# Gated attention and mixer on one core: the queues of the first loads, transposes for the first outputs, and the share of mixer work at the end

## The chip, the cores and the metric

The kernel runs on one core of a Trainium2 chip. The metric is device time in microseconds (us) from start to end of one execution. TensorE (PE) multiplies matrices and writes to the accumulation memory (PSUM); VectorE (DVE) and ScalarE (ACT) work element by element; GpSimd (POOL) and SyncE (SP) here mostly issue transfers. Transfers (DMAs) are issued on the queues of SP, ACT and POOL and all run on the same 16 DMA engines. Each engine works through its own instructions in order, and waits on semaphores for those of others.

## What is computed

Eight batches, each with 3136 rows; u and v have 256 columns, z has 64. All inputs and the output are float32.

```
attn = max(z z^T / S, 0)^2          # 3136 x 3136, symmetric
x    = u * (attn v)                 # gate
h    = V^T (U^T x)                  # low-rank mix over the rows, rank 32
u2   = x + h
out  = u2 + max(u2 w1, 0) w2        # w1: 256 x 1024, w2: 1024 x 256
```

The first two lines are called attention here, the others the mixer. `moe_U`, `moe_V`, `moe_w_ch1` and `moe_w_ch2` are U, V, w1 and w2.

## The kernel before

Rows are cut into 24 blocks of 128 and a tail of 64 (index 24). A score block (i, j) is a 128 x 128 product of z columns (line 881), two running at once in the two halves of TensorE's rows. ScalarE or VectorE applies the relu on the way from PSUM to SBUF (lines 896, 898; 1024 columns at a time as a rule), and VectorE squares it in place (902). Output block c sums 25 products of a score block with a v block (909) in one of two PSUM accumulators (`NACC = 2`), then VectorE multiplies by u (935, "the gate"). The tail's output is summed transposed (917) and turned (927).

The scores are symmetric, so from batch 1 on only blocks with j >= i are computed, and the others are made by a transposing DMA from SBUF to SBUF on SP's queue (905), up to 8 blocks each. In batch 0, where the transposes would come late, the columns 0 to 7 are computed for all rows without transposes (`DIRECT = 8`), and the triangle with transposes begins at column 8. The tail's scores (tile TJ) are always transposed: 12 blocks that each of the outputs 0 to 23 needs once.

The mixer of a batch: t1 = U^T x over the whole batch (944), a copy, then for each of seven groups k of rows (six of 512, a tail): h (963), add (974), cast (755 or 753), a transposing DMA (991), w1 in four parts of 256 columns (1001), relu (1012 on ScalarE, 1014 on VectorE), w2 in two halves of 16 products (1027), add (1039) and a store from POOL's queue (1044). Two output buffers `ob` take turns.

Nothing of this order is written out by hand. `make_plan` lists tasks with engines they may run on, durations, dependencies, buffers to take and priorities, and `Plan.run` plays them through once, at build time; the order in which the tasks start there is the order of the instructions on each engine. A task with two engines goes to the first unless that is behind by more than its `slack`. `behind` means "not before that one has started". `select` chooses TensorE's next task: score blocks up to `LOOK` outputs ahead in bursts, else the next products of an output, else mixer work. Mixer work is taken when its progress lies more than one batch and `HOLD` = 0.12 of a batch behind that of attention.

Start of batch 0: z is loaded by SP and ACT, v by SP and POOL in turn, each v load of two blocks (256 KB) into one of six staging buffers `stg`, from where VectorE or ScalarE casts it to bf16. The first u loads (for outputs 0 to 5 and the tail) and all weight loads go out on POOL's queue: two weight loads after the gate of each of the first six outputs in order, w1 first, then w2, U and V. They are cast from the staging buffers too. The first t1 waits for all weights.

Of the kernel before, what the change touches and what calls it, by code (L numbers as in the profile page):

```python
# [15 lines left out]
P = 128  # L16
NB, S, D, DQK, R, H = 8, 3136, 256, 64, 32, 1024
NT = 24
# [8 lines left out]
DIRECT = 8  # L27
HOLD = 0.12

# [246 lines left out]
def make_plan():  # L276
# [9 lines left out]
    duos, avs = [], []  # L286
    out_done = {}
    after = lambda b, pos: out_done.get((b, pos))
    wts = []
# [6 lines left out]
    for b in range(NB):  # L296
# [45 lines left out]
        for n, k in enumerate([12] + list(range(12))):  # L342
            st = Ref("stg")
            w = 2 if k < 12 else 1
            ld = add(
                f"vld{b}.{k}", {"ACT": 0.5} if b else {("SP", "POOL")[k % 2]: 0.55},
# [36 lines left out]
        tail = [(place[0], True, None, 0), (place[0], True, None, 16)]  # L383
        direct = 0
        if b == 0:

            for s in range(0, DIRECT, 4):
                at = place[s]
                for j in range(s, NT, 2):
                    units.append((at, False, [(j, s, 4), (j + 1, s, 4)]))  # L390
                if s == 0:
                        units += tail
                for c in range(s, s + 4):
                    units += [(place[s + 4], False, x) for x in split(c, s + 4, NT - s - 4)]
            direct = DIRECT
        else:
            units = tail
        for c in range(direct, NT):
            units += [(place[c], True, x) for x in split(c, c, NT - c)]
        small = []  # L400
        for at, turn, parts, *j0 in units:
            al = []
            if parts is None:
# [9 lines left out]
            else:  # L413
# [11 lines left out]
                nt = (t0 + len(tiles) - r0) if turn else 0  # L425
# [21 lines left out]
            if nt:  # L447
                src = [TJ] if parts is None else [refs[r0 - t0 + i] for i in range(nt)]
                x = add(
                    f"tr{b}.{c}.{t0}", {"SP": t_tr(nt)},  # L450
                    lambda K, t, src=src, tb=tb, nt=nt, o=t0 * 64: K.tr_quad(t, src[0], o, tb, nt),
                    deps=[s], prio=0.5, pipe=T_BLK * nt, use=src + tb.refs,
                )
            for n, (r, i) in enumerate(tiles):
                sq[r, i] = s
                if parts is not None:
                    row[r, i] = blk.refs[n]
                    if nt and i >= r0:
# [14 lines left out]
        xs, evs = [], []  # L473
        for pos, c in enumerate(order):
            if c == NT or c % 2 == 0:
                u = Ref("u24" if c == NT else "us")
                uld = add(
                    f"uld{b}.{c}", {"ACT": 0.5} if b or pos > 6 else {"POOL": 0.55}, lambda K, t, b=b, c=c, u=u: K.load_u(t, b, c, u),
                    deps=[after(b, pos - 6) if pos > 6 else after(b - 1, 18 + pos)], prio=3.5, behind=[] if b else vl[-1:],
# [11 lines left out]
            acc = Ref("acc")  # L491
            last, at = None, 0
            for i, seg in enumerate(groups):
# [6 lines left out]
                emit = lambda K, t, seg=seg, acc=acc, v=v, f=first, l=end: K.av(t, seg, acc, v, f, l)  # L500
                if c == NT:
# [4 lines left out]
                    alloc=[acc] if first else [], use=list(refs.values()) + [v] + ([] if first else [acc]),  # L506
                )
                last.b, last.pos, last.n = b, b * 25 + pos, len(seg) * (0.27 if c == NT else 1.0)
# [17 lines left out]
            elif c > 0:  # L526
                x = xs[-1]
            takes = c == NT or c % 4 == 0
            ev = add(
                f"x{b}.{c}", {"DVE": t_dvp(P if c == NT else D)},  # L530
                lambda K, t, c=c, acc=acc, u=u, x=x: K.gate(t, c, acc, u, x),
                deps=[last, uld] + ([] if takes else [evs[-1]]), prio=0.2,
                alloc=[x] if takes else [], use=[acc, u] + ([] if takes else [x]),
            )
            out_done[b, pos] = ev
            evs.append(ev)

            for n in range(2 * pos, min(2 * pos + 2, 12)) if b == 0 else ():
                st = Ref("stg")
                ld = add(  # L540
                    f"wld{n}", {"POOL": 0.6}, lambda K, t, n=n, st=st: K.load_w(t, n, st),
# [559 lines left out]
```

## Time and profile before

| | us |
|---|---|
| median of 5 executions | 1062.05 |
| lowest and highest | 1057.31, 1063.96 |
| the profiled execution | 1063.64 |
| its span, first to last instruction | 1060.7 |
| TensorE busy | 1027.9 |
| VectorE busy | 606.6 |
| ScalarE busy | 482.3 |
| first product with U (batch 0) | at 118.22 |
| first h of the last batch | at 1002.68 |
| last product | ends at 1054.7 |

The busy time of an engine counts its instructions' durations, merged where they overlap; issuing a DMA is not counted as busy. "Idle before" an instruction comes with what ended the idle time. PEld is TensorE's loading of the stationary operand, which runs beside the products. The granted clock is the share of TensorE's full clock that it was given. The DMA share is the mean busy share of the 16 DMA engines; it can exceed 1 where the packets of several queues overlap.

### The profile page before, as it was taken

Reading aid. Unit: us, or ns where it says so; the run is one execution under the profiler, and the core shown is the slowest. Engines: PE = TensorE matmul, PEld = TensorE weight load, DVE = VectorE, ACT = ScalarE, POOL = GpSimd, SP = SyncE. Lnnn points to the kernel's source line nnn. Section 1 sums busy time; section 2 is a strip of 40 time slices with the busy share of each in tenths; the row PEclk is TensorE's granted clock in tenths of the full one; section 3 lists DMA queues with packets and bytes.
Section 4 is the critical chain, followed back from the end, with each engine's and each line's share of the span. In section 5 each row is a group of like instructions: output and inputs, shape, how many; then the busy total and the mean of one; then the engine's idle time right before and its main releaser. Section 6 shows DMA issues by size and latency. Waiting matters only on the chain.

```text
span 1060.7 us, 22216 instructions
## 1 busy us (share of the span) xinstructions
PE 1027.9 (97%) x9100; PEld 770.7 (73%) x9181; DVE 606.6 (57%) x1096; ACT 482.3 (45%) x586; POOL 78.2 (7%) x147
## 2 busy tenths in 40 slices
PE   6999999999999999999999999999999999999997
PEld 3667767877777776777777777777777777777765
DVE  8885755466564665646574646645656475652332
ACT  7773445254543634435344355435444363433253
POOL 2300000000000000000000000000100001000111
PEclk9999999999999999999999999999999999999999
DMA  5789999769995978959799798978889698664132
GB/s 154 195 173 218 200 201 187 168 161 175 192 193 150 192 152 175 199 149 186 158 200 190 159 176 159 213 190 165 165 184 185 164 181 169 135 141 85 46 96 88
DMA packets 404293, 176.85 MB, mean 167 GB/s; under 512 B 368544, under 2 KB 369984, under 8 KB 404192
## 3 DMA queue, kind: packets, MB, share of 16 engines
q1 hardware_dynamic: 363216, 91.19, 51.7%
q10 hardware_dynamic: 30976, 53.23, 19.4%
q0 software_dynamic: 10000, 31.02, 9.3%
q8 instruction: 71, 1.16, 0.5%
q14 instruction: 30, 0.25, 0.1%
HBM read 60.70 MB, written 25.69 MB: 81 GB/s over the span
## 4 chain that ended last, share of the span: by engine, by line
PE 76%; issue 15%; DMA 4%; DVE 2%; POOL 1%; ACT 1%; POOLq 0%; DVEq 0%
PE acc L909 42%; PE pair L1001 12%; PE acc L1027 12%; PE pair L881 7%; PE pair L963 1%; DMA q<-q 1%; POOL out_dram L1044 1%; DMA uT<-ubf 1%; DMA stg<-in_v_dram 1%; PE acc L917 1%; ACT q L896 1%; DVE q L902 1%; DVE q L898 1%; PE acc L1020 0%; PE acc L944 0%
## 5 line engine op out<-in xcount | busy, mean ns | idle before, releaser
L909 PE MATMUL acc<-v,q 128*128 128x256 bf16 x4800 | 590.4, 274 | 8.2 <-DMA q<-q 2.9
L909 PEld LDWEIGHTS <-q 128*128 128x128 bf16 x4800 | 461.5, 98 | 130.2 <-issue 44.1
L896 ACT ACTIVATE q<-pair 128x1024 bf16<-128x1024 f32 (+6 forms) x288 | 229.8, 852 | 269.7 <-PE pair L881 255.3
L1012 ACT ACTIVATE r<-pair 128x1024 bf16<-128x1024 f32 (+1 forms) x197 | 195.7, 1007 | 254.6 <-PE pair L1001 239.9
L902 DVE TENSOR_TENSOR q<-q 128x1024 bf16<-128x1024 bf16 (+7 forms) x402 | 213.5, 574 | 11.2 <-ACT q L896 10.8
L1001 PE MATMUL pair<-uT,w1b 128*128 128x512 bf16 (+1 forms) x815 | 193.9, 353 | 10.8 <-DMA uT<-ubf 6.7
L1027 PE MATMUL acc<-w2b,r 128*128 128x256 bf16 x1536 | 185.0, 274 | 0.1
L1027 PEld LDWEIGHTS <-r 128*128 128x128 bf16 x1536 | 149.5, 98 | 28.1 <-issue 5.7
L935 DVE TENSOR_TENSOR xc<-acc,us 128x256 bf16<-128x256 f32 x192 | 80.8, 421 | 153.9 <-PE acc L909 151.2
L898 DVE TENSOR_SCALAR q<-pair 128x768 bf16<-128x768 f32 (+6 forms) x114 | 112.7, 989 | 75.2 <-PE pair L881 60.6
L1039 DVE TENSOR_TENSOR ob<-acc,u 128x512 f32<-128x512 f32 (+1 forms) x104 | 68.6, 659 | 132.1 <-PE acc L1027 128.2
L1001 PEld LDWEIGHTS <-w1b 128*128 128x128 bf16 x896 | 79.4, 98 | 63.3 <-DMA uT<-ubf 5.2
L1044 POOL DMA_DIRECT2D out_dram<-ob x96 | 52.2, 543 | 926.7 <-DVE ob L1039 861.5
L881 PE MATMUL pair<-zT 64*128 64x512 bf16 (+4 forms) x972 | 103.4, 317 | 2.4 <-DVE q L898 1.3
L974 DVE TENSOR_TENSOR u<-pair,xc 128x1024 f32<-128x1024 f32 x48 | 58.6, 1222 | 37.6 <-PE pair L963 24.7
L881 PEld LDWEIGHTS <-zT 64*128 64x128 bf16 x972 | 32.1, 94 | 44.4 <-issue 34.5
L755 DVE CAST v<-stg 128x512 bf16<-128x512 f32 (+1 forms) x71 | 28.9, 409 | 12.9 <-DMA stg<-in_v_dram 12.9
L755 DVE CAST ubf<-u 128x1024 bf16<-128x1024 f32 x41 | 28.2, 688 | 6.1 <-DMA uT<-ubf 3.4
L963 PE MATMUL pair<-t,Vb 128*128 128x256 bf16 x192 | 28.5, 273 | 0.1
L963 PEld LDWEIGHTS <-Vb 128*128 128x128 bf16 x192 | 18.7, 98 | 4.3
L753 ACT CAST v<-stg 128x512 bf16<-128x512 f32 (+1 forms) x33 | 19.7, 600 | 3.8 <-DMA stg<-in_v_dram 2.6
L917 PEld LDWEIGHTS <-v 128*128 128x128 bf16 x400 | 13.6, 98 | 3.1 <-issue 1.9
(68 smaller groups left out, 180.7 us busy)
## 6 DMA issues: line engine op xcount, KB each, us to landing
out_dram<-ob POOLq DMA_DIRECT2D x96, 256.0 KB, 2.9
us<-in_u_dram ACTq DMA_DIRECT2D x93, 256.0 KB, 3.4
stg<-in_v_dram ACTq DMA_DIRECT2D x84, 256.0 KB, 3.4
stg<-in_z_dram ACTq DMA_DIRECT2D x22, 256.0 KB, 3.3
q<-q SPq DMA_TRANSPOSE x352, 3.8
stg<-in_moe_w_ch_dram POOLq DMA_DIRECT2D x8, 256.0 KB, 4.8
stg<-in_v_dram SPq DMA_DIRECT2D x6, 256.0 KB, 4.2
stg<-in_v_dram POOLq DMA_DIRECT2D x6, 256.0 KB, 4.4
```

The costliest lines, as they stand in the source:

```text
L881: self.nc.tensor.matmul(out=ps[:, h, pc : pc + w], lhsT=z[a, r * P : (r + 1) * P], rhs=z[a, c0 : c0 + w], start=True, stop=True,)
L896: self.nc.scalar.activation(out=o, in_=i, func=AF.Relu)
L898: self.nc.vector.tensor_single_scalar(out=o, in_=i, scalar=0.0, op=ALU.max)
L902: self.nc.vector.tensor_tensor(out=o, in0=o, in1=o, op=ALU.mult)
L909: self.nc.tensor.matmul(out=self.acc[acc.i][:, :D], lhsT=self.q[:, ref.i, :], rhs=self.v[v.i][:, j, :], start=first and n == 0, stop=last ...
L935: self.nc.vector.tensor_tensor(out=o, in0=i0, in1=i1, op=ALU.mult)
L974: self.nc.vector.tensor_tensor(out=o, in0=i, in1=x, op=ALU.add)
L1001: self.nc.tensor.matmul(out=o, lhsT=self.w1b[:, e, ht * P : (ht + 1) * P], rhs=r, start=e == 0, stop=e == ND - 1)
L1012: self.nc.scalar.activation(out=o, in_=i, func=AF.Relu)
L1027: self.nc.tensor.matmul(out=self.acc[acc.i][:, w * D : (w + 1) * D], lhsT=self.r1[r1s[ht // 2].i][:, ht % 2, (2 * h + w) * P : (2 * h + w ...
L1039: self.nc.vector.tensor_tensor(out=o, in0=i, in1=x, op=ALU.add)
L1044: self.q_of(t).dma_start(out=self.rows("out", b, t0, t0 + 2), in_=self.ob[ob.i])
```

## The change

It has these parts.

- **Weights**: issued on ScalarE's queue and not on POOL's, after later outputs (positions 4 to 9 of batch 0's order 0, 1, 2, 3, tail, 4, 5, ...), in the order U, V, w1, w2. Each piece of V is a task of its own. t1 waits for U only, h for V, w1 for w1, w2 for w2.
- **First loads**: all v blocks 0 to 11 and the tail through staging buffers on SP. Blocks 12 to 23 by three loads of four blocks on POOL's queue, which cast to bf16 on the way (`load_v_bf`) and need no staging buffer and no cast; a copy of one element on POOL (`gate_v`), which waits for the second cast, stands before them. The first u loads go out on SP right after v.
- **Scores of batch 0**: for columns 0 to 3 all 24 rows are computed as before; of the blocks (0 to 3, j), those for j from 4 to 15 are now made by DMA transposes of these (`FLIP = 16`), those for j from 16 computed. For the columns 4 to 7, 8 to 11 and 12 to 15 the transposes serve the rows up to 13, 17 and 21 (`DIRECT = (0, 14, 18, 22)`), and the rest is computed. The number of score blocks of batch 0 goes from 456 to 410, that of transposed blocks (with the tail's 12) from 132 to 178, in 37 DMAs where there were 25.
- **Outputs 0 to 3**: outputs 2 and 3 are summed in the second half of the accumulators of 0 and 1 (`d0`), so that all four are open at the same time. Each gate waits for both sums of its bank.
- **End**: in the last batch the mixer is held back by `HOLD_LAST` = 0.2 of a batch in place of 0.12, and the relu of w1 goes to VectorE when ScalarE is behind by 0.2 us in place of 1.0. Of its 25 relus in the last batch 6 are then VectorE's, before none. Between w1 (or w2) tasks of one group the plan waits for the start of the one before, no longer for its end.

```diff
-DIRECT = 8
+DIRECT = (0, 14, 18, 22)
+WAT = [(n, 4 + k // 2) for k, n in enumerate((8, 9, 10, 11, 0, 1, 2, 3, 4, 5, 6, 7))]
+GATE_V = 1
+FLIP = 16
 HOLD = 0.12
+HOLD_LAST = 0.2
...
+            if b == 0 and 6 <= k < 12:
+                if k % 2 == 0:
+                    if k == 6:
+                        c = add(
+                            f"vg{b}", {"POOL": 0.1}, lambda K, t, v=v: K.gate_v(t, v),
+                            deps=[vc[GATE_V]], prio=0.1, use=[v], lat=0.1,
+                        )
+                        vgate = [c]
+                    c = add(
+                        f"vx{b}.{k}", {"POOL": 0.6}, lambda K, t, k=k, v=v: K.load_v_bf(t, k, v),
+                        deps=vgate, behind=[vc[k - 1]] if k > 6 else [], prio=0.2, pipe=T_ROW * 4, use=[v],
+                    )
+                vc[k] = c
+                continue
...
-                f"vld{b}.{k}", {"ACT": 0.5} if b else {("SP", "POOL")[k % 2]: 0.55},
+                f"vld{b}.{k}", {"ACT": 0.5} if b else {"SP": 0.5},
...
+        for c in range(NT):
+            lim, s = NT, c // 4
+            if b == 0 and s < len(DIRECT):
+                lim = DIRECT[s]
+                if c % 4 == 0:
+                    for j in range(lim, NT, 2):
+                        units.append((place[c], 0, [(j, c, 4), (j + 1, c, 4)], 4 <= j < FLIP and s == 0))
+                if c == 0:
+                    units += tail
+            if lim == 0:
+                units += [(place[4], 0, x) for x in split(c, FLIP, NT - FLIP)]
+            else:
+                units += [(place[c], lim, x) for x in split(c, c, NT - c)]
...
-                nt = (t0 + len(tiles) - r0) if turn else 0
+                nt = len(tiles) if flip else max(0, min(t0 + len(tiles), lim) - r0)
...
-                    f"uld{b}.{c}", {"ACT": 0.5} if b or pos > 6 else {"POOL": 0.55}, lambda K, t, b=b, c=c, u=u: K.load_u(t, b, c, u),
+                    f"uld{b}.{c}", {"ACT": 0.5} if b or pos > 6 else {"SP": 0.5}, lambda K, t, b=b, c=c, u=u: K.load_u(t, b, c, u),
...
+            quad = b == 0 and c < 4
+            share = quad and c >= 2
+            acc = quads[c - 2][1] if share else Ref("acc")
+            d0 = D if share else 0
...
-            for n in range(2 * pos, min(2 * pos + 2, 12)) if b == 0 else ():
+            for n in [n for n, at in WAT if at == pos] if b == 0 else ():
                 st = Ref("stg")
-                ld = add(
-                    f"wld{n}", {"POOL": 0.6}, lambda K, t, n=n, st=st: K.load_w(t, n, st),
-                    deps=[ev], prio=0.5, pipe=0.8 if n < 8 else 0.5, alloc=[st] + tok(True),
-                )
                 for g in range(4 if n == 10 else 3 if n == 11 else 1):
+                    ld = add(
+                        f"wld{n}.{g}", {"ACT": 0.5 if n < 10 else 0.4}, lambda K, t, n=n, g=g, st=st: K.load_w(t, n, g, st),
+                        deps=[ev], behind=[] if g == 0 else [ld], prio=0.45, pipe=0.8 if n < 8 else 0.5 if n < 10 else 0.2,
+                        alloc=([] if g else [st]) + tok(True), use=[st] if g else [],
+                    )
...
-            deps=evs + (wts if b == 0 else []), kind="mix", alloc=[acc], use=xs + [x24],
+            deps=evs + need(8, 9), kind="mix", alloc=[acc], use=xs + [x24],
...
-                ), 1.0))
+                ), 1.0 if b < NB - 1 else 0.2))
...
-            pick = mx if mx.work == 0 or st["mix"] / MIX < st["att"] / ATT - 1.0 - HOLD else av
+            pick = mx if mx.work == 0 or st["mix"] / MIX < st["att"] / ATT - 1.0 - (HOLD if av.b < NB - 1 else HOLD_LAST) else av
...
+    def load_v_bf(self, t, k, v):
+        self.q_of(t).dma_start(
+            out=self.v[v.i][:, 2 * k : 2 * k + 4, :], in_=self.rows("v", 0, 2 * k, 2 * k + 4)
+        )
+
+    def gate_v(self, t, v):
+        w = self.v[v.i]
+        self.nc.gpsimd.tensor_copy(out=w[:1, NT // 2, :1], in_=w[:1, 2 * GATE_V, :1])
...
-                out=self.acc[acc.i][:, :D], lhsT=self.q[:, ref.i, :], rhs=self.v[v.i][:, j, :],
+                out=self.acc[acc.i][:, d0 : d0 + D], lhsT=self.q[:, ref.i, :], rhs=self.v[v.i][:, j, :],
```

## The prediction

> **What bounds the kernel now.** I read the page's busy line first, then TensorE's waits, then busy times by stage, then the timeline where the stages were poor.
>
> ```profile
> PE 1027.9 (97%) x9100; PEld 770.7 (73%) x9181; DVE 606.6 (57%) x1096; ACT 482.3 (45%) x586; POOL 78.2 (7%) x147
> ```
>
> TensorE is busy nearly all the time, so only its stalls and its slow stretches can be won. The waits of TensorE name them (total us, times, longest):
>
> ```profile
> PE pair L1001 <- DMA uT<-ubf: 6.7, 3, 2.4
> ...
> PE acc L909 <- DMA q<-q: 2.9, 4, 1.4
> PE acc L909 <- DVE v L755: 2.2, 2, 2.0
> PE acc L909 <- ACT v L753: 2.0, 1, 2.0
> ```
>
> About 14 us in all, in three places: v arriving late at the start, transposes of scores late around 62 us, transposes for the mixer late three times. The stages of the start (columns: window, length, busy us and instructions of PE, PEld, DVE, ACT, POOL, granted TensorE clock, DMA share, GB/s):
>
> ```profile
> core 0: us, PE busy (x) PEld busy (x) DVE busy (x) ACT busy (x) POOL busy (x), PEclk, DMA share, GB/s
> ...
> 22.00:31.00 9.00, 6.80 (x47) 3.74 (x47) 7.13 (x13) 5.48 (x8) 5.17 (x9) 0.83 1.06 150
> ...
> 45.00:62.00 17.00, 17.00 (x146) 11.37 (x143) 16.03 (x28) 14.58 (x21) 3.67 (x7) 1.00 0.47 114
> 62.00:70.00 8.00, 5.70 (x38) 3.59 (x36) 7.28 (x16) 6.10 (x8) 0.00 (x0) 0.79 1.04 219
> 70.00:118.20 48.20, 47.64 (x472) 37.19 (x469) 32.97 (x66) 21.08 (x27) 0.00 (x0) 1.00 1.13 215
> ```
>
> In 22 to 31 us everybody waits and DMA is full; in 45 to 62 DMA is half empty while all engines work; in 62 to 70 DMA is full and TensorE stalls. What ends the first stage (timeline: start, length, instruction, wait):
>
> ```profile
> 29.99 0.62 ACT L753 CAST v<-stg 128x512 bf16<-128x512 f32 x1 [2.31 <-DMA stg<-in_v_dram]
> ...
> 30.66 0.81 PE L909 MATMUL acc<-v,q 128*128 128x256 bf16 x6 [1.96 <-ACT v L753]
> ...
> 32.72 4.17 PE L909 MATMUL acc<-v,q 128*128 128x256 bf16 x25
> ```
>
> The last v tiles are cast at 30.6 us, since a load waits for a staging buffer and a buffer for a cast. Output 3 then still needs all its 25 products and ends at 36.9 us. They take 4.17 us where 25 elsewhere take 2.90: the clock was halved. Clock windows show when that happens (PE busy, clock, DMA):
>
> ```profile
> core 0: us, PE busy (x), PEclk, DMA share, GB/s
> 62.20:66.10 3.90, 1.68 (x15) 1.00 1.01 212
> 66.10:69.50 3.40, 3.32 (x16) 0.50 1.05 223
> ...
> 137.10:139.60 2.50, 0.06 (x2) 1.00 1.48 80
> 139.60:143.00 3.40, 3.35 (x27) 1.00 1.14 256
> ```
>
> 3.4 us at clock 0.50 lose 1.7 us. Near the end the same pair stands again:
>
> ```profile
> 1004.87 1.04 PE L963 MATMUL pair<-t,Vb 128*128 128x256 bf16 x8
> 1008.14 0.61 PE L1001 MATMUL pair<-uT,w1b 128*128 128x512 bf16 x1 [2.23 <-DMA uT<-ubf]
> ```
>
> **The clock, row against rule.** By rows, of six stalls of about 2 us (1.98 at 19.4, 1.96 at 28.7, 1.38 plus 0.91 at 62, 2.44 at 137, 2.06 at 405, 2.23 at 1006) five are followed by 3.4 us at 0.50, so a removed stall brings 1.7 us more. The Trainium skill, "TensorE: Matmul & The Clock Gate", Part 1, lets the clock fall only after at least one idle window of about 3.4 us; then none of these would cost clock. The trace differs and decides: with it my sum below is 13.4 us, by the page it would be about 10.
>
> **Part 1, the first four outputs, to 36.9 us.** Before, two accumulators serve outputs 0 and 1, then 2 and 3. Now each bank holds two outputs side by side, so each arriving v tile is used by all four, and the 50 products of 2 and 3 no longer follow the last arrival. v tiles 12 to 23 go past staging and cast: three casting loads of 512 KB on POOL's queue, behind one 1-element copy that waits for the second cast. Their speed is in no row. Bounds: v, z and u are 0.80+3.21+0.83 = 4.8 MB; at the 215 GB/s of the first 15 us they are in at 22.5, at the 296 of 30 to 40 us at 16. The plain 256 KB v loads on POOL land in 4.4 us (median); u loads there beside transposes in 9.3. I take 20 us for the last v tile.
>
> A rule speaks against the POOL queue: the Trainium skill, "SBUF — State Buffer", section "SBUF: two separate sides", says that a 2-port VectorE operation keeps GpSimd from writing descriptors; its section on the wrong intuition has a load of 620 ns take 3100. The row for POOL's v loads, issued among VectorE's casts (ns, min/median/max):
>
> ```profile
> L804 POOL DMA_DIRECT2D stg<-in_v_dram x6: 536/538/956, 5.6 to 22.1; - x6
> ```
>
> By the row three issues cost 1.6 us, by the page (estimate) 9.3, and the last v would come at 28 instead of 20. Even that is hidden, because another arrival is later: the tail's transposes. The tail closes each of the four sums, and six new transposes of 8 blocks (FLIP: rows 4 to 15 against columns 0 to 3) stand before them on SP, with five u issues (0.3 us each) too. Price of a block: in 110 to 120 us, DMA full of transposes,
>
> ```profile
> q1 hardware_dynamic: 6854, 1.70, 97.3%
> ```
>
> 1.70 MB / 32 KB = 52 blocks in 10 us, 0.19 us each. 48+12 blocks are 11.5 us; after loads that end about 19, 30.5. Bounds: 12+11.5 = 23.5 if loads cost them nothing, so v decides; and 40 if the 4.2 MB left at 12 us crawl at the 150 GB/s of 22 to 31, where two transposes beside POOL loads took this long (us):
>
> ```profile
> DMA to landing us min/median/max: 8.2/9.4/10.6
> ```
>
> I take 30.5, plus four closing products and latency: 31.5 against 36.9, **-5.4**.
>
> **Part 2, to 118.2 us** (the first product with U). Output 4 onward used no transposes up to output 7; then 120 blocks were wanted at once, issued from 60.55 on. Now 30 blocks go early for each group of four, in the half-empty stretch. The 1.38+0.91 stall and its slow clock go: **-4.0**. Score blocks of batch 0 fall from 456 to 410 (128 columns each, two at once: 26.7 ns): **-1.2**. Relu and square of 46 blocks (5.75 units of 1.0 and 0.66 us) and six v casts leave ScalarE and VectorE; TensorE is full in 45 to 62, so worth nothing itself. It pays for what is added: 18 weight issues on ScalarE at 0.34 = 6.1 us, and eight more weight casts there. Without that cover ScalarE's idle 4.3 us (45 to 70) would be overdrawn by about 2 and scores late by as much. New wait: both banks close together, so the tail output waits for two gates (0.42 each, between other VectorE work); 0 to 3, I take **+1.5**. The u loads come 15 us earlier; the 2.1 us that VectorE waited for u lies beside TensorE's wait, counted already. Weights are loaded later, but U is wanted at 118 and w1 at 139 us: hidden by over 40 us. Shorter waits of t1, h, w1, w2 on weights: 0 by the same cover. Batch 0 ends 5.4+4.0+1.2-1.5 = **9.1 us** earlier.
>
> **Part 3, the middle**: same work, other order. The two stalls at 137 and 405 (2.4; 2.1 plus clock 1.7) may go or new ones come: 0, from -6 to +4.
>
> **Part 4, the end.** With HOLD_LAST the built order has 16+16+16 products of batch 6 and four of h between the last batch's first h and its first w1 (about 4.9 us), before 16 and eight (3.0). The chain h, add, cast, transpose takes 1002.68 to 1008.14, 5.5 us. Stall 2.45 to 0.3: -2.1; slow clock: -1.7. Six of the 25 last relus move to VectorE (15.5 busy of 47 us): 0. The last but one product group is now a full one and the tail's store starts before it, so the last add should not wait its 0.7 us for a store: -0.5. Sum **-4.3**.
>
> **Sum**: -9.1-4.3 = -13.4 on the profiled execution of 1063.64 (span 1060.7 plus 2.9 around it), which stands 1.6 above the median: 1062.05-13.4 = 1048.7, say **1049**.
>
> **Rivals.** *DMA takes it back* (0.18): 46 more blocks are 8.7 us of transposes, and 70 to 118 already runs at share 1.13; transposes beside POOL loads crawl. Then the first four outputs end at 37 to 40 or outputs 8 to 23 wait, and only the end's 4.3 stays: 1058. Against it: the blocks go into a stretch at 0.47. *The middle's stalls go too* (0.10): -6, 1043. *Slower* (0.07): ScalarE issues in order, and each weight load waits for a gate, a staging buffer and an older load; relus stand behind it, and TensorE's next products behind those. POOL stood 13 us at these waits, where it harmed nobody. ScalarE can give 4.3. At 0.98 us of wait an issue (17.7 us) the gain of 13.4 is gone; at 1.6, 18 x 1.6 - 4.3 - 13.4 = +11: 1073. Against it: ScalarE's 40 separate waits before v loads have median 17 and maximum 38 ns. *The casting loads or the shared banks do nothing*, as transposes end the stage anyway, and gates cost 3 (0.03): 1059.
>
> **How the numbers follow.** The forecast has 0.62, its own range 1043 to 1055 (gates, tail transposes). Over all cases 1040 to 1060 leaves out the slower case and a little of both sides. A measurement here tells about 0.5% (5.3 us) from nothing: faster means below 1056.7. The forecast gives 0.61, the second rival 0.10, a milder first one 0.07: faster 0.78, same 0.14, slower 0.08.
>
> **What would show it.** Output 3's last product near 31 us; no TensorE wait on v over 1 us; no wait on q<-q near 62; first product with U near 109; wait on uT near the end under 0.5 us and clock 1.00 there. ScalarE idle before weight issues between 38 and 75 us would prove the slower rival; tail transposes landing past 36 us the first.

## The result, and the profile after

| | before | after |
|---|---|---|
| median of the runs on one chip, us | 1060.48 (79 runs) | 1062.34 (44 runs) |
| the profiled execution, us | 1063.64 | 1060.03 |
| its span, us | 1060.7 | 1058.2 |
| first product with U, at us | 118.22 | 114.30 |
| first product with U of the last batch, at us | 999.21 | 991.01 |
| last product ends, at us | 1054.72 | 1046.43 |
| from there to the end of the span, us | 6.0 | 11.8 |

The ratio is 1.0015, with a 95% interval of 1.0004 to 1.0026: if anything slower by 1.6 us, where the prediction said 1049 (13.4 us less). Two of the 44 executions after, at 1072.6 and 1073.0 us, were slow ones and count in the median but not in the ratio.

Two cautions go ahead of any reading. The profiled execution of before was 3.2 us slower than its own median and that of after 2.3 us faster than its own, so side by side the two profiles flatter the change by 5.5 us. And executions of one kernel are spread over some 15 us, so a moment in a single profile may be off by a few us. What is stated about an edit's worth therefore rests on timed runs; the profiles say where to look.

The busy line of after, to be read against that of before: TensorE is busy 7.4 us less. That isn't 7.4 us less work. The score blocks saved are 1.2 us; the rest is the clock, which up to the last product was at 0.50 for 3.4 us five times in the profile of before and once in that of after, at 1.7 us each.

```profile
PE 1020.5 (96%) x9091; PEld 768.1 (73%) x9171; DVE 617.2 (58%) x1094; ACT 466.8 (44%) x572; POOL 63.6 (6%) x122
```

The waits of TensorE (total us, times, longest):

```profile
PE acc L964 <- DMA q<-q: 5.5, 7, 1.4
PE pair L936 <- ACT q L951: 5.0, 7, 1.8
...
PE acc L972 <- DVE xc L990: 1.9, 1, 1.9
PE pair L1056 <- DMA uT<-ubf: 1.3, 2, 0.8
```

The two waits for v are gone, and that for uT fell from 6.7 to 1.3. Three are new or larger: transposes of scores (5.5 after 2.9), relus on ScalarE (5.0 after 0.8), and the tail's output, which waits for the two gates.

The stages of the start, with the columns of before (window, length, busy us and instructions of PE, PEld, DVE, ACT, POOL, clock, DMA share, GB/s):

```profile
core 0: us, PE busy (x) PEld busy (x) DVE busy (x) ACT busy (x) POOL busy (x), PEclk, DMA share, GB/s
...
22.00:31.00 9.00, 7.93 (x66) 4.59 (x64) 7.86 (x13) 7.27 (x9) 0.00 (x0) 1.00 0.75 146
31.00:37.00 6.00, 3.76 (x57) 2.62 (x55) 5.84 (x12) 4.58 (x6) 0.00 (x0) 0.79 0.62 69
...
45.00:62.00 17.00, 15.32 (x127) 10.40 (x128) 13.25 (x19) 9.54 (x12) 0.00 (x0) 1.00 0.87 179
62.00:70.00 8.00, 7.22 (x66) 5.84 (x66) 6.55 (x13) 7.53 (x10) 0.00 (x0) 1.00 0.54 120
70.00:118.20 48.20, 43.78 (x461) 34.26 (x458) 33.30 (x68) 19.57 (x29) 0.00 (x0) 1.00 1.16 222
```

TensorE does better than before in 22 to 31 us (7.93 busy at clock 1.00, before 6.80 at 0.83), and in 62 to 70 too. But 45 to 62, where it was busy for all of 17.00, and 70 to 118, where it was busy for 47.64 of 48.20, now have gaps: what was gained first is idled away later.

The closing instructions of the program stand on one line of their own. This is that line's answer for POOL in before (ns, minimum/median/maximum, first and last start):

```profile
L1096 POOLq DRAIN  x3: 51/102/3477, 1056.4 to 1060.4; - x3
```

and in after:

```profile
L1151 POOLq DRAIN  x3: 51/93/10029, 1047.4 to 1058.0; - x3
```

POOL ends the program with a drain, and everything waits for that. It took 3.48 us before and 10.03 us after, from 1047.4 to 1057.5, although the last bytes of the output landed at about 1049.5. This is where to look for the gain of the end; the experiments below show that it was lost there.

### The profile page after: what moved, and what is told of

It reads as the page before. It is cut to its first block, busy times and chain, and to the rows that moved or that the text cites. A ratio compares the mean times of both kernels' runs of the same rounds, so it can differ in the third digit from the quotient of the medians.

```text
span 1058.2 us, 22190 instructions
## 1 busy us (share of the span) xinstructions
PE 1020.5 (96%) x9091; PEld 768.1 (73%) x9171; DVE 617.2 (58%) x1094; ACT 466.8 (44%) x572; POOL 63.6 (6%) x122
## 4 chain that ended last, share of the span: by engine, by line
PE 89%; DMA 4%; DVE 3%; issue 2%; ACT 1%; ACTq 0%; POOL 0%; POOLq 0%; SPq 0%; DVEq 0%
PE acc L964 46%; PE pair L1056 15%; PE acc L1082 15%; PE pair L936 7%; DMA q<-q 3%; PE pair L1018 2%; PE acc L972 1%; DVE q L953 1%; DMA uT<-ubf 1%; DMA stg<-in_v_dram 1%; DVE q L957 1%; PE acc L1075 1%; PE acc L999 1%; ACT q L951 1%; ACT Vb L800 0%
## 5 line engine op out<-in xcount | busy, mean ns | idle before, releaser
L964 PE MATMUL acc<-v,q 128*128 128x256 bf16 x4800 | 582.9, 273 | 5.9 <-DMA q<-q 5.5
L951 ACT ACTIVATE q<-pair 128x1024 bf16<-128x1024 f32 (+6 forms) x274 | 218.7, 849 | 248.7 <-PE pair L936 209.7
L1067 ACT ACTIVATE r<-pair 128x1024 bf16<-128x1024 f32 (+1 forms) x186 | 182.7, 1005 | 265.5 <-PE pair L1056 260.3
L957 DVE TENSOR_TENSOR q<-q 128x1024 bf16<-128x1024 bf16 (+7 forms) x397 | 210.5, 571 | 20.7 <-ACT q L951 19.8
L1056 PE MATMUL pair<-uT,w1b 128*128 128x512 bf16 (+1 forms) x816 | 186.7, 350 | 5.7 <-DMA uT<-ubf 1.3
L1082 PE MATMUL acc<-w2b,r 128*128 128x256 bf16 x1536 | 182.4, 273 | 0.5 <-DVE ob L1094 0.4
L953 DVE TENSOR_SCALAR q<-pair 128x768 bf16<-128x768 f32 (+7 forms) x123 | 120.5, 984 | 72.5 <-PE pair L936 66.1
L936 PEld LDWEIGHTS <-zT 64*128 64x128 bf16 x962 | 31.9, 94 | 46.8 <-issue 36.8
L802 DVE CAST v<-stg 128x512 bf16<-128x512 f32 (+1 forms) x74 | 29.5, 404 | 20.0 <-DMA stg<-in_v_dram 19.9
L1069 DVE TENSOR_SCALAR r<-pair 128x1024 bf16<-128x1024 f32 x14 | 17.1, 1224 | 16.5 <-PE pair L1056 14.3
L802 DVE CAST ubf<-u 128x1024 bf16<-128x1024 f32 x37 | 25.4, 687 | 0.5
L800 ACT CAST ubf<-u 128x1024 bf16<-128x1024 f32 x11 | 11.5, 1042 | 18.0 <-DMA uT<-ubf 9.9
```

What stands on the lines that cost most here:

```text
L936: self.nc.tensor.matmul(out=ps[:, h, pc : pc + w], lhsT=z[a, r * P : (r + 1) * P], rhs=z[a, c0 : c0 + w], start=True, stop=True,)
L951: self.nc.scalar.activation(out=o, in_=i, func=AF.Relu)
L953: self.nc.vector.tensor_single_scalar(out=o, in_=i, scalar=0.0, op=ALU.max)
L957: self.nc.vector.tensor_tensor(out=o, in0=o, in1=o, op=ALU.mult)
L964: self.nc.tensor.matmul(out=self.acc[acc.i][:, d0 : d0 + D], lhsT=self.q[:, ref.i, :], rhs=self.v[v.i][:, j, :], start=first and n == 0, s ...
L1056: self.nc.tensor.matmul(out=o, lhsT=self.w1b[:, e, ht * P : (ht + 1) * P], rhs=r, start=e == 0, stop=e == ND - 1)
```

## The experiments

All ratios are to the kernel before, run beside on the same chip; those of different experiments come from four chips. A difference of two ratios has an uncertainty of its own: for most pairs below some 0.2 to 0.3%, or 2 to 3 us. "Transfers" are the DMAs that POOL issues in one execution, counted in the trace: 141 before, 115 after.

### The last stores on SP

For this experiment the stores of the last batch's groups 4 to 6 go out on SP's queue, first in the changed kernel and then in the kernel before, so that POOL is done early and its drain can run beside the last products.

```diff
-                    f"st{b}.{k}.{h}", {"POOL": 0.6},
+                    f"st{b}.{k}.{h}", {"SP": 0.6} if b == NB - 1 and k >= 4 else {"POOL": 0.6},
```

After the change:

> The changed kernel, with the last batch's stores of groups 4 to 6 issued on SP's queue and not on POOL's. In its profile the last product ended at 1046.4 us, 8.3 earlier than before, but POOL's closing drain ran from 1047.4 to 1057.5 and the span ended behind it. Theory 1: the drain follows POOL's last store and is what the gain went into; with no store on POOL in the last 15 us it runs beside products, the span ends 3 to 4 us after the last product, and the time falls by 5 to 8 us, to about 1055. Theory 2: products do not end earlier in most executions, and the drain is no loss; then the time stays within 2 us of the change's 1062.

Measured: 0.9954 [0.9938, 0.9971], 1052.96 us against 1057.8.

Before the change:

> The kernel before, with the same stores of the last batch on SP's queue. Its drain ran from 1056.4 to 1059.9, only about 1.5 us past the landing of the last store. Theory 1: the time falls by 1 to 2 us only. Theory 2 (the drain costs both kernels alike in most executions): it falls by as much as the changed kernel does.

Measured: 0.9985 [0.9973, 0.9997], 1056.17 us. POOL's drain in the changed kernel with this edit:

```profile
L1151 POOLq DRAIN  x3: 51/102/9529, 1032.5 to 1051.0; - x3
```

It still takes 9.53 us, but starts at 1032.5, and the span ends 4.1 us after the last product (11.8 in after). The same edit brings 0.61% there (1.0015 to 0.9954) and 0.15% in the kernel before, both as their first theories had it. The difference, 0.46% or 4.9 us (give or take 2.5), is what the change lost at POOL's drain. With the drain out of the way in both, the change takes 0.9985 to 0.9954: a gain of 0.31% (3.3 us, give or take 2.2), not 13.4.

### More transfers on POOL

If the drain's length comes from how many transfers POOL has issued, transfers that nobody needs should shorten it. Twelve loads of 16 bytes a partition are issued in batch 3; nobody reads what they bring. The last stores stay on POOL.

```diff
+            if b == 3:
+                n = t0 // 2
+                self.nc.gpsimd.dma_start(out=self.pad[:, n, :], in_=self.rows("z", 0, n, n + 1)[:, 0, :4])
```

> The changed kernel with 12 loads of 16 bytes a partition added on POOL's queue during batch 3; they fill a tile that nobody reads. POOL's closing drain against the number of transfers that POOL issued, so far: 141: 3.5 us, 135: 3.2, 115: 10.0, 112: 9.8, 109: 9.5. Theory A: the drain works through what POOL's queue holds since a ring of it last came round (0.08 us a transfer), and that happens between 115 and 135; with 127 the drain is back at 2.5 to 3.5 us and the time falls by about 6 us, though work was added. Theory B: it grows with the number alone and something else shortened it before; then 11 us and no gain. Theory C: casting loads or the moved weights lengthen it: 10 us.

Measured: 0.9933 [0.9908, 0.9958], 1053.72 us against 1060.76 (six executions). By *adding* twelve transfers the changed kernel lost 0.8% of its time; Theory A's short drain came true, and B and C fall. The drain (the line's number is 4 higher here):

```profile
L1155 POOLq DRAIN  x3: 51/93/2933, 1047.2 to 1050.7; - x3
```

With six loads (121 transfers):

> The changed kernel with 6 instead of 12 tiny unread loads on POOL's queue in batch 3 (121 transfers in all from POOL in place of 115). Theory R (what POOL's last drain costs grows with the transfers since a round number of descriptors was passed[...]): 121 transfers pass it, the drain is 2.2 to 2.6 us, shorter than the 2.93 with 127, and the end is as with 12 loads (span near 1051). Rival (the drain has its step elsewhere between 121 and 127): it is 10.3 to 10.6 us, and the span near 1059.

One execution: 1057.34 us, span 1055.6.

```profile
L1155 POOLq DRAIN  x3: 51/102/2677, 1052.1 to 1055.3; - x3
```

The drain is short with 121 (2.68, a little over Theory R's 2.6), and the rival's 10.3 falls. Theory R's reason, a count of descriptors, is no part of what the run shows. And the span was 4.6 us over what Theory R said: 2.1 of that stand before the last product, the rest in POOL. POOL's timeline of this run shows its very last store held for something that the profile doesn't name (the release is given as "issue"):

```profile
1047.62 0.57 POOL L1100 DMA_DIRECT2D out_dram<-ob  x1 [1.07 <-DVE ob L1095]
1052.12 0.56 POOL L1100 DMA_DIRECT2D out_dram<-ob  x1 [3.92 <-issue]
```

With this in mind I looked for the same mark at the stores of the others. The kernel before has it once, at its 122nd transfer; the add that makes the data is shown with it:

```profile
984.92 0.69 DVE L1039 TENSOR_TENSOR ob<-acc,u 128x512 f32<-128x512 f32 x1 [1.74 <-PE acc L1027]
988.67 0.55 POOL L1044 DMA_DIRECT2D out_dram<-ob  x1 [16.05 <-issue]
```

and the kernel with twelve loads at its 120th:

```profile
1032.51 1.07 POOL L1100 DMA_DIRECT2D out_dram<-ob  x2 [7.84 <-issue]
```

All seven kernels with 121 transfers or more show one such hold, at transfer 120 to 122, and a closing drain of 2.7 to 3.5 us. All seven with 115 or fewer show no hold and a closing drain of 9.5 to 10.0 us. The number in brackets is not the length of the hold, as most of it is time in which the store's data wasn't there yet. In the kernel before the data's add ends at 985.61, and the store goes out 3.06 us later; a store goes out 0.29 us after its add as a rule. In all seven kernels the held store goes out 3.02 to 3.07 us after its add. So the hold costs that one store about 2.8 us: in the kernel before in the middle of the last batch, where TensorE waits for no store. In the changed kernel, with 26 transfers fewer, there is no hold, but a drain 6.5 us longer, where everybody waits. What POOL does in the hold and in the drain, and why the one comes with the shorter other, no run shows.

### Without the casting loads

v blocks 12 to 23 staged and cast like the others, all on SP's queue.

```diff
-            if b == 0 and 6 <= k < 12:
+            if b == 0 and 99 <= k < 12:
```

> The changed kernel without the casting loads and the one-element copy: all of v through staging buffers on SP, so POOL issues nothing but stores. If the casting loads or the copy lengthen POOL's closing drain, the drain is back at about 3.5 us. If it is the late end of two full stores in a row, the drain stays near 10 us. For the start: the last v cast comes about 5 us later than the casting loads landed, and output 3 ends 2 to 5 us later, since transposes stand behind v in SP's queue.

Measured: 1.0081 [1.0053, 1.0108], 1065.66 us (six executions). POOL now issues stores alone (112), and its drain is 9.79 us, so neither the casting loads nor the copy before them make it long. The start is worse: in its profile the products of outputs 0 to 3 end at 33.75 us, 2.8 later than in after, and the first product with U comes at 122.15, with one wait of 8.8 us for a gate at 89 us. Against the change (1.0015) the casting loads with their copy are worth 0.7%.

### Without the one-element copy

The casting loads start at once and not behind the second cast.

```diff
-                        c = add(
-                            f"vg{b}", {"POOL": 0.1}, lambda K, t, v=v: K.gate_v(t, v),
-                            deps=[vc[GATE_V]], prio=0.1, use=[v], lat=0.1,
-                        )
-                        vgate = [c]
+                        vgate = []
```

> The changed kernel without the one-element copy on POOL; the casting loads start at once. Theory 1a, a compute instruction late in POOL's life makes the drain long: drain back at 3.5 us. Theory 1b, casting loads make it long: drain stays at 10 us. The first z and v loads share the DMA engines with the casting loads from 1 us on, so the first score blocks come 1 to 3 us later.

Measured: 1.0085 [1.0062, 1.0109], 1066.45 us (four executions). POOL's drain is 10.03 us, as with the copy, so Theory 1a falls; that casting loads make it long (1b) had been refuted by the run before. The casting loads no longer wait until the first v blocks are there: TensorE waits 4.2 us for z's transposes, output 3's products end at 37.5 us as before the change, and the first product with U comes at 124.38. Against the change (1.0015) holding back these large loads is worth 0.7% (7.4 us, give or take 2.8). That they compete with z for the DMA engines is how I read it; the profile doesn't split that wait.

### Without the transposes for columns 0 to 3

```diff
-FLIP = 16
+FLIP = 4
```

This stands on the changed kernel with its last stores on SP; 48 blocks are computed and not transposed.

> The changed kernel with its last stores on SP, and no transposes of the blocks (columns 0 to 3, rows 4 to 15): FLIP is 4 and these 48 blocks are computed, as before the change. Prediction's reckoning (the transposes lie in a stretch with room): 48 blocks at 26.7 ns are 1.3 us more of TensorE, first product with U at 116, 1054.3 (0.9967). Rival (six transposes of 8 blocks ahead of the tail's, and their relus on ScalarE and VectorE, cost the start as much as they save): the tail's transposes land some 6 to 9 us earlier, but the 48 blocks need six more relus and squares ahead of output 3; first product with U within 1 us of 114.7, and 0.993 to 0.996.

Measured: 1.0004 [0.9985, 1.0023], 1060.48 us: 0.5% (5.3 us, give or take 2.7) slower than with the transposes (0.9954). Both theories fall: the transposes cost the start nothing on balance that computing would save, and they save some four times the 1.3 us of products that the prediction counted. The profile shows where. Without them outputs 0 to 3 are done earlier still, at 28.4 us, but then both supplying engines are full (after has VectorE 5.37 and ScalarE 3.90 here):

```profile
37.00:45.00 8.00, 5.87 (x27) 2.02 (x27) 7.96 (x16) 7.51 (x10) 0.00 (x0) 0.60 0.29 60
```

Later TensorE waits 3.5 us for a transpose at 60 us and 3.5 us for transposes of z near 105, each with a slow clock behind it. The first product with U comes at 124.2, where the theories had 116 and 114.7. That the extra relus and squares push those transposes back is argued, not shown.

### The weight loads back on POOL

The changed kernel with its last stores on SP, and the weight loads on POOL's queue; order and places as changed.

```diff
-                        f"wld{n}.{g}", {"ACT": 0.5 if n < 10 else 0.4}, lambda K, t, n=n, g=g, st=st: K.load_w(t, n, g, st),
+                        f"wld{n}.{g}", {"POOL": 0.6}, lambda K, t, n=n, g=g, st=st: K.load_w(t, n, g, st),
```

> The changed kernel with the last stores on SP (the drain out of the way, 1053 us beside 1058 for before), and its weight loads back on POOL's queue, in the new order and at the new places. Theory 1: the relus behind weight issues on ScalarE are what held TensorE up between 43 and 112 us (TensorE waited 6.5 us for them there, 0.8 in the kernel before); then these waits fall under 2 us, the first product with U comes 2 to 4 us earlier than 114.5, and the time falls by 1 to 4 us. Theory 2: VectorE and ScalarE are short of time there whoever issues; then waits and time stay within 1 us.

Measured: 0.9929 [0.9903, 0.9954], 1053.18 us (six executions). With the weights on ScalarE it was 0.9954 [0.9938, 0.9971] on another chip: the intervals overlap. The waits of TensorE:

```profile
PE acc L964 <- DVE xc L990: 3.6, 2, 3.3
PE acc L964 <- DMA q<-TJ: 3.0, 1, 3.0
...
PE pair L936 <- ACT q L951: 0.8, 2, 0.5
```

The wait for ScalarE's relus falls from 6.5 us (with the weights on ScalarE) to 0.8, and 6.6 us of waits for gates and for the tail's transposes stand in its place. The first product with U comes at 118.2, not 2 to 4 us earlier than 114.5 as Theory 1 had it (some 1.3 us of that are products that this order puts before it). The last product ends at 1046.50, against 1047.21 with the weights on ScalarE. So the waits for ScalarE went and others came. The time may be up to 6 us better or the same: the runs don't part Theory 1's 1 to 4 us from nothing.

### V cast on VectorE

On the way to 62 us three casts of V stand in a row on ScalarE. Its timeline in after, and TensorE's next product behind them:

```profile
58.14 3.99 ACT L800 CAST Vb<-stg 32x504 bf16<-32x504 f32 x3
...
62.77 0.34 PE L936 MATMUL pair<-zT 64*128 64x384 bf16 x2 [1.80 <-ACT q L951]
```

1.33 us each; VectorE took 0.71 for such a cast before. These casts are fixed to VectorE, with the weight loads on POOL (first) and with them on ScalarE (second).

```diff
-                        f"wc{n}.{g}", {"DVE": t_dve(512), "ACT": t_act(512)},
+                        f"wc{n}.{g}", {"DVE": 0.72} if n >= 10 else {"DVE": t_dve(512), "ACT": t_act(512)},
```

> As the kernel with weights on POOL, and the seven casts of V on VectorE alone, where one takes 0.71 us and not 1.33 as on ScalarE. If three such casts in a row (4.0 us at 58) were what held up the relus, the stall of 1.8 to 2.1 us at 58 to 61 is gone here and stays in the kernel with the weights on POOL; time 0 to 2 us below that one. If the issues held them up, the two are alike.

Measured: 0.9957 [0.9941, 0.9973], 1056.41 us, on the chip where the kernel with the weights on POOL had 0.9929. The stall at 58 to 61 us was already gone there, so this run doesn't tell casts from issues.

> The changed kernel with its last stores on SP, and the seven casts of V (wc10, wc11) fixed to VectorE; nothing else by hand, though the planner may reorder what follows. In the changed kernel ScalarE takes three of them in a row at 58 to 62 us, 1.33 us each, and TensorE waits 1.8 to 2.1 us for the relu behind them; VectorE needs 0.71 us each. Theory W (these casts on ScalarE are a cause of the small gain): the wait on ScalarE's q near 60 us falls under 0.5 us, first product with U about 2 us earlier (112.7), 0.9935 of the kernel before. Rival (TensorE is short of scores from several sides at once, and another wait takes its place): waits up to the first product with U within 1.5 us of 9.0 in sum, first product with U from 114 to 116, 0.994 to 0.997.

Measured: 0.9943 [0.9925, 0.996], 1054.86 us, against 0.9954 without. In neither is there a gain beyond the intervals. The profiled execution of the second was the slowest of its 21 (1063.34), so its moments count little; its waits from 31 us up to the first product with U still show the kind of trade:

```profile
PE acc L964 <- DMA q<-q: 9.2, 4, 4.5
PE acc L972 <- DVE xc L990: 1.9, 1, 1.9
PE pair L936 <- ACT q L951: 1.5, 2, 1.2
```

The wait for ScalarE went from 5.2 to 1.5 us, and that for transposes rose from 3.8 to 9.2. That is the kind of thing the rival said, and the time lies in its range (0.994 to 0.997), though also in reach of Theory W's 0.9935. Its other figures were off: these two waits are 10.7 us in sum where it had 9.0, and the first product with U came at 121.8 (with 37 products of the tail more before it than in after), where it had 114 to 116.

### The end alone, from both sides

The changed kernel with its last stores on SP, and the end of before:

```diff
-HOLD_LAST = 0.2
+HOLD_LAST = 0.12
...
-                ), 1.0 if b < NB - 1 else 0.2))
+                ), 1.0))
```

> The changed kernel with the last stores on SP, HOLD_LAST at 0.12 and the slack of the last relus at 1.0, as before. If the end was worth what the two profiles show, the wait for the first uT of the last batch is back at 2.2 us, with a slow clock behind it, and the time rises by 3 to 4 us. If it was worth nothing, the time stays within 1 us.

Measured: 1.0003 [0.9982, 1.0024], 1060.55 us. The wait for the first uT is 4.40 us, twice the 2.2 expected, and the time rises by 5.2, not 3 to 4.

And the kernel before, its start untouched, with the end of the changed one and its last stores on SP:

```diff
+HOLD_LAST = 0.2
...
-                ), 1.0))
+                ), 1.0 if b < NB - 1 else 0.2))
...
-            pick = mx if mx.work == 0 or st["mix"] / MIX < st["att"] / ATT - 1.0 - HOLD else av
+            pick = mx if mx.work == 0 or st["mix"] / MIX < st["att"] / ATT - 1.0 - (HOLD if av.b < NB - 1 else HOLD_LAST) else av
```

> The kernel before, with two things of the changed one's end alone: the mixer held back by 0.2 of a batch in the last batch (and its relu given to VectorE at 0.2 us), and the last batch's stores of groups 4 to 6 on SP so that no closing work of POOL is in the way. The start of batch 0 is untouched. Theory S (the start parts bring nothing, the end part is the whole gain of the work before the last product): 0.9985 of the kernel before for the stores alone, less 0.5% for the end: 0.993 to 0.995, equal to or below the changed kernel with the same stores (0.9954); no wait over 1 us on uT in the last 60 us. Rival (the start parts do carry a gain of about 3 us, the end about 3): 0.9955 to 0.998.

Measured: 0.9964 [0.9949, 0.9978], 1056.40 us. No wait for uT near the end is over 1 us. But the time lies in the range of the rival (0.9955 to 0.998) and above that of Theory S (0.993 to 0.995).

Four ratios, all with the last stores on SP, belong together here:

| | end of before | end of the change |
|---|---|---|
| start of before | 0.9985 | 0.9964 |
| start of the change | 1.0003 | 0.9954 |

On the new start the end is worth 0.5% (5.2 us, give or take 2.8), on the old one 0.2% (2.2, give or take 2.0). With the changed end the start is worth 0.1% (1.1, give or take 2.3), with the old end it costs 0.2% (1.9, give or take 2.6). So a start worth 9 us is excluded, and with the changed end one worth 3 is not; that the end carries the gain and the start next to nothing is likely, not shown. Nor do the two rows differ by the start alone: the third piece of the end (w1 and w2 tasks wait for the start of the one before) works in all batches, stays in both kernels of the lower row and is missing in the upper one. No run takes it out alone.

TensorE's products behind the last batch's first h, in the changed kernel with the old end:

```profile
1002.26 1.47 PE L1018 MATMUL pair<-t,Vb 128*128 128x256 bf16 x12
1008.13 0.61 PE L1056 MATMUL pair<-uT,w1b 128*128 128x512 bf16 x1 [4.40 <-DMA uT<-ubf]
```

and in after:

```profile
993.17 0.60 PE L1018 MATMUL pair<-t,Vb 128*128 128x256 bf16 x4
993.61 3.66 PE L1082 MATMUL acc<-w2b,r 128*128 128x256 bf16 x32
997.10 1.06 PE L1075 MATMUL acc<-w2b,r 128*128 128x128 bf16 x16
998.00 0.60 PE L1018 MATMUL pair<-t,Vb 128*128 128x256 bf16 x4
999.37 3.61 PE L1056 MATMUL pair<-uT,w1b 128*128 128x512 bf16 x15 [0.77 <-DMA uT<-ubf]
```

The work kept back, 48 products of w2, now stands between the first h and the first w1, and the wait for uT is 0.77 us where it was 4.40 (2.23 in before). All three profiles with the old end have a stretch at clock 0.50 behind this wait, and none of the eleven with the new end has one there.

## Why the prediction was wrong

**Part 1 was right.** The products of outputs 0 to 3 end at 30.9 us (predicted 31.5, before 36.9), and at 29.5 to 32.1 in the four other profiles with this start. The casting loads take 0.55 to 0.68 us to issue (predicted 1.6 for three) and land in 6.4 to 8.7 us, near 20 as taken; the tail's transposes were the last to land, near 30. The row for POOL's issues held. The slower price of the Trainium skill, "SBUF — State Buffer", section "A bandwidth-pool intuition that's wrong (but worth ruling out)", didn't come up, although VectorE cast v from 8.1 to 17.0 us; whether these casts are of the kind that the page means, no run here shows.

```profile
L858 POOL DMA_DIRECT2D v<-in_v_dram x3: 552/557/678, 9.8 to 11.0; - x3
```

**Part 2 failed.** Two of its terms were wrong: the -4.0 for "The 1.38+0.91 stall and its slow clock go", with the two gates as the only new wait; and that relief and new load of ScalarE and VectorE cancel, as TensorE "is full in 45 to 62". The windows up to output 3's last product, and from there to the first product with U, in before:

```profile
0.00:37.00 37.00, 25.14 (x175) 13.77 (x177) 28.88 (x61) 25.85 (x33) 11.66 (x25) 0.91 0.72 182
37.00:118.20 81.20, 78.35 (x751) 57.56 (x747) 63.69 (x122) 48.45 (x60) 5.75 (x11) 0.98 0.93 191
```

and in after:

```profile
0.00:31.00 31.00, 23.94 (x196) 14.49 (x197) 24.32 (x49) 21.96 (x26) 2.68 (x10) 1.00 0.89 196
31.00:114.30 83.30, 72.91 (x683) 54.64 (x680) 60.42 (x117) 42.56 (x55) 0.00 (x0) 0.98 0.97 185
```

Idle time of TensorE is window less busy: 11.86 and 2.85 us before, 7.06 and 10.39 after. The first window gained 4.8, the second lost 7.5. The 7.5 are waits for transposes (4.2 us in all behind 31 us, before 2.9), for relus (4.2, before none) and for the two gates (1.9, where +1.5 was predicted). The outputs 0 to 3 are done six us earlier, but the scores of the outputs behind them are not: the supply (relu, square, transpose) set the pace, and TensorE waits for it a little later. So the stall near 62 us didn't go, it changed its cause. All five profiles with this start have one between 56 and 63: four times 1.5 to 2.1 us for the relu behind the three casts of V on ScalarE, once 3.0 us for a transpose. Three of the five have the slow clock behind it. The profile of after is one of the two that don't, which was luck. Here is the stretch in the kernel with its last stores on SP, in that with twelve loads and in that with six:

```profile
core 0: us, PE busy (x), PEclk, DMA share, GB/s
60.50:63.80 3.30, 3.30 (x17) 0.50 0.00 0
64.10:67.40 3.30, 3.30 (x18) 0.50 0.19 27
59.30:62.60 3.30, 3.30 (x18) 0.50 0.95 248
```

The experiments with weights on POOL and V on VectorE each took one wait away and got another.

**The milestone was not like for like.** The predicted "first product with U near 109" took everything before that product to be batch 0's. In the built order of before, 25 tail products and 41 blocks' worth of scores that stand before it are gone from there in the changed kernel and come after it (11,136 columns of scores fewer before it, of which the change saves 5,888; the rest is only moved). 41 blocks at 26.7 ns are 1.1 us and 25 tail products at 33 to 58 ns 0.8 to 1.4: about 2 us. With it the busy time agrees: it fell by 103.48 - 96.84 = 6.6, made of 1.2 (score blocks, as predicted), about 3.4 (two slow stretches of the clock less) and about 2 that was only put off. The 3.9 us in the table are thus some 1.9 of gain, in a pair of profiles that flatters the change. More profiles say less: the three with the old start have this product at 116.3, 117.0 and 118.2, the five with the new one at 113.7 to 116.0 (median 114.7). That is 2.3 us between the medians, of which about 2 were put off. The timed runs give 1.1.

**The clock.** The row held, not the window of 3.4 us of the Trainium skill, "TensorE: Matmul & The Clock Gate", Part 1: in after the wait of 1.86 us at 31.9 is followed by a slow stretch (0.79 in 31 to 37). The slow stretches of before at 66.1, 407 and 1008 us are missing in it. But the row only tells what a stall costs once it is gone, and near 62 us one stayed.

**Part 3**, 0 with -6 to +4, can't be settled from single profiles: two profiles of kernels with the same middle (before, with its stores on POOL and on SP) differ by 2.6 us from the first product with U of batch 0 to that of batch 7. The table has this stretch 4.3 us shorter after, but `HOLD_LAST` moves mixer work behind its end: with the new end it is 874.9 us on the old start and 876.7 to 877.7 on the new one in four profiles, which fits the 2 us that batch 0 put off.

**Part 4 was right in its mechanism for TensorE**: the wait and its slow clock went. Its size is open (-3.8 predicted for TensorE; 5.2 us measured on this start, 2.2 on the old). **It was wrong in its last line**: "-0.5" for a store that no longer waits. What lies behind the last product grew from 6.0 to 11.8 us, by POOL's drain. No rival had it; I took the closing 6 us of the span as fixed.

Put together, from the timed runs: start -1.1 (predicted -9.1), end -2.2 without the start's help (predicted -3.8), drain +4.9 (predicted -0.5 there): +1.6. Of the 15.0 us between this and the -13.4 the start makes 8.0, the drain 5.4 and the end 1.6. That the sum is the 1.0015 of the result is no check, since the three are differences along one chain of ratios that ends there; each is uncertain by 2 to 2.5 us. The end is worth more on the new start than on the old (5.2 against 2.2), or, said the other way, the start is worth nothing with the old end: these are one observation. With the old end and the new code the wait for uT is 4.40 us, longer than the 2.23 of before, so that pairing is worse than either kernel's own.

The last rival, *the casting loads or the shared banks do nothing*, had the time nearest (1059), and *DMA takes it back* came next (1058), but neither had the place: outputs 0 to 3 were done early, and transposes made only part of the waits behind. The rival *Slower* had ScalarE's queue as its cause; taking the weight loads off it changed the time by no more than the intervals.

Of the versions tried, six beat the kernel before by 0.4 to 0.7%, each with the drain short or out of the way: last stores on SP (0.9954), the same with weights on POOL (0.9929), with V on VectorE (0.9943) or with both (0.9957), the kernel before with the new end (0.9964), and twelve idle transfers on POOL (0.9933). Their intervals overlap, so none of them is shown to be the best. The kernel before with its last stores on SP has 0.9985.

## What to carry to other kernels

Read what stands behind the last product, line by line, before you take the end of the span as fixed, and ask of every transfer that is moved to another queue what the old queue does at its end. When a milestone is compared between two orders of work, count what each order puts before it; work that is moved past it looks like a gain. Before a stall that is missing in one profile is called gone, look at a second profile of the same order. And where one engine is full and those that feed it nearly so, taking one wait away may only bring up the next: a timed run of each piece tells what it is worth.

## What the runs showed of the hardware

- With 109 to 115 transfers issued by POOL in one execution, its closing drain took 9.5 to 10.0 us: 9.53 with 109, 9.79 with 112, 10.03 with 115, or 0.083 us a transfer. With 121 to 141 it took 2.7 to 3.5 us, and one store, transfer 120 to 122, went out 3.0 us after its data was made in place of 0.3. Between 115 and 121 no run was made. Two kernels with the same number can differ a little (127: 2.93, 3.02 and 3.19).
- A drain that starts 15 us before the last product is done costs nothing: with the last stores on SP it ran from 1032.5 to 1042, and the last product ended at 1047.2. Where the hold falls on the very last store (121 transfers), it stands in everybody's way like the drain.
- A cast of V, 32 partitions by 504 columns with a step between the columns read, took 1.33 us on ScalarE and 0.71 us on VectorE; one of v, 128 partitions by 512 in a row, took 0.62 and 0.42. Whether the step makes the difference, no run shows.
- A one-element copy that holds three casting loads back until the first v blocks have been cast was worth 0.7%: without it TensorE waits 4.2 us for the transposes of z.
